# Grouped-query decode attention on one core: half of the first values between the first keys, the last pair's values in the loop

## The chip, the cores and the metric

The kernel runs on one core of a Trainium2 chip. The metric is the device time of one execution in microseconds (us). The core has TensorE (matrix products), VectorE, ScalarE and GpSimd (elementwise work, reductions, copies), SyncE (which here issues nearly all transfers) and 16 DMA engines that move data between the chip's HBM memory and the core's SBUF. TensorE writes its results to PSUM.

## The reference

One query token attends to 65,536 keys. There are 32 query heads and 8 key and value heads, so 4 query heads share each key head; a head has 128 elements, all in bf16.

```
scale = D ** -0.5                                   # D = 128
scores = jnp.einsum("bhqd,bhkd->bhqk", q, k) * scale
p = _softmax(scores, axis=-1)
return jnp.einsum("bhqk,bhkd->bhqd", p, v)          # k, v repeated 4 times over heads
```

Keys and values are 134 MB each; every byte is used once, for four queries.

## The kernel before, in words

**Tiles.** A head's 65,536 keys are cut into 4 units of 16,384 keys. A unit lies in SBUF as 128 partitions by 128 tiles (T) of 128 elements: 4.19 MB. Two units are a *pair*; there are 16 pairs (NP), two per head. Below, Kp and Vp are the keys and the values of pair p, and a and b their first and second unit.

**Buffers.** `kbuf` holds two units, `vbuf` two, `bbuf` one. A pair's keys are loaded as one transfer into kbuf (pairs 1 to 14, `WHOLE`), and GpSimd (6 of 8 blocks, L223) and ScalarE (2 blocks, L347) copy the second unit from kbuf to bbuf, so that kbuf comes free for the next pair's keys early. Pairs 0 and 15 are loaded a unit at a time, straight to kbuf's first half and to bbuf.

**One lap of a pair.** TensorE transposes each key tile (L138) so that the head's elements lie along the partitions, eight tiles at a time; VectorE (three of four groups, L217) and ScalarE (one of four, L215) move the transposed tiles from PSUM to SBUF; TensorE multiplies them with the four queries (L149). VectorE takes the maximum over the pair (L237), GpSimd over partitions (L386); ScalarE takes the exponentials (L340) into `pts`, and their sums. After the keys of a lap, TensorE multiplies the exponentials of the *previous* pair with its values (`pe_values`, L154 to L161): 256 products in one PSUM group, opened by the first product. So V(p) is used in lap p+1. VectorE then adds the PSUM result to the head's running sum `acc`: a copy for the first pair of a head (L281), a product with alpha, the correction for a new maximum (L294), an addition for the second pair (L285), and the division by the sum of exponentials (L286).

**The loop and what follows it.** TensorE's loop has 16 laps (L195). It skips the values in lap 0. The last pair's values come behind the loop, in code of their own (`pe_last_values`, L163 to L175), from kbuf; there the running sum enters the PSUM group as a product with an identity matrix (L169). Ahead of the loop are 48 small products (`PE_LEAD`, L190).

**Order of the transfers.** SyncE's program is written out (L433 to L447) and is executed in order: a wait holds up all that is behind it. The transfers run in one queue, in order of issue. The order is K0 in four pieces, K1, V0, K2, V1, and so on to K15, V14, V15. Each is held by a wait: K(p) for `kfree` (L409), three tokens per pair: one when the first unit has been transposed, one from GpSimd and one from ScalarE when their copies are done; a unit into bbuf for `bfree`, when bbuf has been transposed; V(p) for `vfree` (L430), when the values before it have been summed. V15 goes into kbuf, its second unit in four pieces (`L_PIECES`, 78, 32, 13 and 5 tiles), so that little work is left behind the last one. The results of 7 heads are stored from `orow`, those of the last head from `lrow` (L447).

Of the kernel before, what the change touches and what calls it, by code (L numbers as in the profile page):

```python
# [7 lines left out]
ALU = mybir.AluOpType  # L8
# [3 lines left out]
T = 128  # L12
# [4 lines left out]
LAG = 3  # L17


PE_LEAD = 48  # L20
CB = 16
HU = 4
Q = 32


K_PIECES = ((64, 64), (64, 64))
L_PIECES = ((128,), (78, 32, 13, 5))

# [11 lines left out]
def starts(sizes):  # L42
    return [sum(sizes[:i]) for i in range(len(sizes))]


def take(e, sem, n=1):

    e.wait_ge(sem, n)
    e.sem_inc(sem, -n)  # L49


def bass_standalone__gqa_softmax__decode_kernel(nc, q, k, v, out):
    _, Hq, _, D = q.shape
    _, H, Sk, _ = k.shape
    R = Hq // H
# [13 lines left out]
    def sem(name):  # L69
        return S(nc.semaphore(name))  # L70
# [36 lines left out]
    qps = pvb[1][:, :].bitcast(DT.bfloat16)  # L107

    kp = [[sem(f"kp{i}_{p}") for p in range(len(K_PIECES[i]))] for i in range(2)]
    vp = sem("vp")  # L110
    lvp = [[sem(f"lvp{i}_{p}") for p in range(len(L_PIECES[i]))] for i in range(2)]

    kfree, bfree = sem("kfree"), sem("bfree")
    cpg, cpa, pgo = sem("cpg"), sem("cpa"), sem("pgo")
# [36 lines left out]
        if j == G - 1:  # L151
            ins.then_inc(qkd, 1)

    def pe_values(pe):  # L154
        vv = vbuf[:, :].rearrange("p (t d) -> p t d", d=D)
        take(pe, vp, 16)
        for n in range(2):
            for t in range(T):
                ins = pe.matmul(pvb[0][:, 0:R], lhsT=vv[:, n * T + t, :], rhs=pts[n][:, t * R:(t + 1) * R],  # L159
                                start=n == 0 and t == 0, stop=n == 1 and t == T - 1)  # L160
            ins.then_inc(pvd if n else pfree, 1)  # L161

    def pe_last_values(pe):  # L163
        vv = kbuf[:, :].rearrange("p (t d) -> p t d", d=D)
        for n in range(2):
            pe.wait_ge(exd, n + 1)
            if n:
                pe.wait_ge(acr, H)
                pe.matmul(pvb[1][:, 0:R], lhsT=identf[:, :], rhs=acc[:, :], start=False, stop=False)  # L169
            for t in range(T):  # L170
                if t in starts(L_PIECES[n]):
                    pe.wait_ge(lvp[n][starts(L_PIECES[n]).index(t)], 16)
                ins = pe.matmul(pvb[1][:, 0:R], lhsT=vv[:, n * T + t, :], rhs=pts[n][:, t * R:(t + 1) * R],  # L173
                                start=n == 0 and t == 0, stop=n == 1 and t == T - 1)
        ins.then_inc(pvd, 1)  # L175

    def pe_keys(pe):
        pend = []
# [9 lines left out]
    def tensor_engine(pe):  # L188
        pe.wait_ge(t_id, 1)
        for _ in range(PE_LEAD):  # L190
            pe.matmul(pvb[0][0:R, 0:R], lhsT=ident[:, 0:R], rhs=ident[:, 0:R], start=True, stop=True)
        pe.wait_ge(q_sem, 16)
        pe.transpose(qps[:, 0:HR], qsb[:, :], ident[0:HR, 0:HR]).then_inc(s_x, 1)
        pe.wait_ge(t_if, 1)
        with pe.Fori(0, NP) as lap:  # L195
            pe_keys(pe)
            with pe.If(lap > 0):
                pe_values(pe)
        pe_last_values(pe)
        pe.wait_ge(t_f, 1)  # L200
        pe.transpose(trb[0][0:R, 0:P], oT[:, HR - R:HR], ident[:, :]).then_inc(s_x, 1)  # L201

# [62 lines left out]
    def dve_pair(e, second, lap):  # L265

        for n in range(2):
            for j in range(G):
                if not on_act(j):
                    evict(e, n, j)  # L270
                if n == 0 and j == 0:
                    e.sem_inc(pgo, 1)
        pair_max(e)
        if second:
            next_queries(e)
        else:
            e.sem_inc(qrdy, 1)
        new_max(e, second)
        if second:
            values_done(e)  # L280
            own(e, e.tensor_copy(acc[:, :], pvb[0][:, 0:R]), xd)  # L281
        else:
            with e.If(lap > 0):
                values_done(e)
                own(e, e.tensor_tensor(acc[:, :], acc[:, :], pvb[0][:, 0:R], ALU.add), xd)  # L285
                own(e, e.tensor_tensor(oT[:, HR - R:HR], acc[:, :], recip[:, :], ALU.mult), xd)  # L286
                own(e, e.tensor_copy(otmp[:, 0:HR - R], oT[:, R:HR]), xd)
                own(e, e.tensor_copy(oT[:, 0:HR - R], otmp[:, 0:HR - R]), xd)
                e.transpose(orow[:, :], oT[:, :]).then_inc(t_o, 1)
        take(e, sx)  # L290
        if not second:
            own(e, e.tensor_tensor(lp[:, :], rsum[:, 0:R], rsum[:, R:2 * R], ALU.add), xd)
            return
        own(e, e.tensor_tensor(acc[:, :], acc[:, :], alpha[:, :], ALU.mult), xd)  # L294
        own(e, e.tensor_tensor(lp[:, :], lp[:, :], alpha[:, :], ALU.mult), xd)
        for n in range(2):
            own(e, e.tensor_tensor(lp[:, :], lp[:, :], rsum[:, n * R:(n + 1) * R], ALU.add), xd)
        e.sem_inc(acr, 1)
        e.sem_inc(lrd, 1)
        take(e, lra)  # L300
        own(e, e.reciprocal(recip[:, :], la[:, :]), xd)
# [16 lines left out]
    def vector_engine(e):  # L318
        make_identity(e)
        e.memset(oT[:, :], 0.0)  # L320
        e.memset(dm[:, :], 0.0)
        e.wait_ge(s_x, 1)
        own(e, e.tensor_copy(qT[:, :], qps[:, 0:HR]), xd)
        next_queries(e)
        with e.Fori(0, H) as lap:
            dve_pair(e, False, lap)
            dve_pair(e, True, lap)
        e.wait_ge(pvd, 1)
        e.tensor_tensor(oT[:, HR - R:HR], pvb[1][:, 0:R], recip[:, :], ALU.mult).then_inc(t_f, 1)  # L329
        e.wait_ge(s_x, 2)  # L330
        e.tensor_copy(lrow[:, :], trb[0][0:R, 0:P]).then_inc(t_row, 1)  # L331

# [11 lines left out]
    def act_pair(e, lap):  # L344

        def copy(o, i):
            return e.activation(o, i, AF.Copy)  # L347

        for j in (3, 7, 11, 15):
            evict(e, 0, j)  # L350
            if j in ACT_COPIES:
                copy_unit(e, (lap - (WHOLE[0] - 1)) * (WHOLE[1] - lap) > 0, ACT_COPIES[j], copy, cpa, xa)
                if j == max(ACT_COPIES):
                    e.sem_inc(kfree, 1)
        for j in (3, 7, 11, 15):
            evict(e, 1, j)
        for n in range(2):
            take(e, pfree)
            exps(e, n)
        take(e, dmr)  # L360
        e.activation(alpha[:, :], dm[:, :], AF.Exp, scale=1.0).then_inc(sx, 1)
# [29 lines left out]
    def sync_engine(e):  # L391
        W = T * D

        def src(x, p):
            h, c = p // 2, p % 2
            return x[h, c * 2 * P * T:(c + 1) * 2 * P * T, :].rearrange("(p t) d -> p (t d)", p=P)

        def pieces(to, s, sizes, sems):
            for a, w, sm in zip(starts(sizes), sizes, sems):
                e.dma_start(to[:, a * D:(a + w) * D], s[:, a * D:(a + w) * D]).then_inc(sm, 16)  # L400

        def tokens(sems):
            for sm in sems:
                e.sem_inc(sm, 16)

        def keys(p):
            ks = src(kf, p)
            if p:
                e.wait_ge(kfree, 3 * p)  # L409
            if WHOLE[0] <= p < WHOLE[1]:  # L410
                e.dma_start(kbuf[:, :], ks).then_inc(kp[0][0], 16)
                tokens(kp[0][1:])
                e.wait_ge(bfree, p)
                tokens(kp[1])
                return
            for n in range(2):
                if n and p:
                    e.wait_ge(bfree, p)
                to, s = bbuf if n else kbuf, ks[:, n * W:(n + 1) * W]
                if p == 0:  # L420
                    pieces(to, s, K_PIECES[n], kp[n])
                else:
                    e.dma_start(to[:, 0:W], s).then_inc(kp[n][0], 16)
                    tokens(kp[n][1:])
            e.sem_inc(cpg, len(POOL_COPIES))
            e.sem_inc(cpa, len(sum(ACT_COPIES.values(), ())))

        def values(p):
            if p:
                e.wait_ge(vfree, p)  # L430
            e.dma_start(vbuf[:, :], src(vf, p)).then_inc(vp, 16)

        keys(0)  # L433
        for p in range(1, NP):
            keys(p)
            values(p - 1)
        e.wait_ge(kfree, 3 * NP)
        vs = src(vf, NP - 1)
        for n in range(2):
            pieces(kbuf[:, n * W:(n + 1) * W], vs[:, n * W:(n + 1) * W], L_PIECES[n], lvp[n])  # L440
        e.wait_ge(t_o, H - 1)
        for b, rows in enumerate(OUT_ROWS):
            for r, n in zip(starts(rows), rows):
                e.dma_start(of[r:r + n, b * Q:(b + 1) * Q],
                            orow[b * Q + r:b * Q + r + n, :]).then_inc(o_sem, 16)
        e.wait_ge(t_row, 1)
        e.dma_start(of[HR - R:HR, :], lrow[:, :]).then_inc(l_sem, 16)  # L447
# [37 lines left out]
```

## Time and profile before

| What | Value |
|---|---|
| Time, median of 3 runs | 628.31 us (628.17 to 630.41) |
| Profiled execution: time, and its span | 630.51 us, 629.1 us |
| TensorE, VectorE, ScalarE, GpSimd busy | 77%, 49%, 37%, 26% of the span |
| Moved by DMA | 268.60 MB, 427 GB/s over the span |
| Granted TensorE clock, mean | 0.774 |

The span is the time from the first to the last instruction that the profiler saw. A group of instructions is named by the line that issued it, the engine, and the tiles that it writes and reads; a "busy" TensorE may still wait inside. "q1" and so on are DMA queues; "instruction" queues carry the engines' code. The letter q behind an engine's name (SPq) is its sequencer, which issues transfers and holds waits.

### The profile page before, as it was taken

To read this page: it belongs to the slowest core of one execution; us is meant where nothing else is said; L and a number is where in the kernel's file an instruction comes from. 1 tells how busy PE (TensorE), PEld (TensorE's weight loads), DVE (VectorE), ACT (ScalarE), POOL (GpSimd) and SP (SyncE) were. 2 spreads that over 40 slices of the span, in tenths; PEclk is the share of its full clock that TensorE was granted. 3 is DMA by queue.
4 is the path that set the end of the run, shared out by engine and by line. 5 is a ranking of instruction groups with operands and counts; after the bars stand their busy time and mean duration, and the time that the engine had idled before them with its cause. 6 is when DMAs were issued, how large, how long until landed. Compare 5 with 4: busy or idle time off the path is not lost. (4 is left out here: it accounts for less than half of the span.)

```text
span 629.1 us, 27597 instructions
## 1 busy us (share of the span) xinstructions
PE 483.7 (77%) x12340; PEld 479.1 (76%) x12340; DVE 306.2 (49%) x608; ACT 234.2 (37%) x431; POOL 165.0 (26%) x114
## 2 busy tenths in 40 slices
PE   5749869497695967949689494995949859599975
PEld 5749869497695967949689494994949859499965
DVE  4627447173461735627355372643717437174730
ACT  2235333263432634325243252433525334253321
POOL 0007051060611506024070340703307042070000
PEclk9958769596695967859678596786959869597975
DMA  8999999999999999999999999999999999999996
GB/s 367 428 419 434 433 438 429 438 433 433 433 433 429 446 421 446 425 442 425 442 425 442 425 442 425 442 425 442 425 442 425 442 429 438 429 421 430 454 405 277
DMA packets 5994, 268.60 MB, mean 427 GB/s; under 512 B 864, under 2 KB 992, under 8 KB 1120
## 3 DMA queue, kind: packets, MB, share of 16 engines
q1 hardware_dynamic: 5936, 268.45, 99.0%
q8 instruction: 8, 0.13, 0.1%
q10 hardware_dynamic: 48, 0.01, 0.0%
q14 instruction: 2, 0.02, 0.0%
HBM read 268.44 MB, written 0.01 MB: 427 GB/s over the span
## 5 line engine op out<-in xcount | busy, mean ns | idle before, releaser
L217 DVE COPY ktb<-trb 128x1024 bf16<-128x1024 bf16 x384 | 257.1, 692 | 169.4 <-PE trb L138 166.7
L138 PE MATMUL trb<-ident,kbuf 128*128 128x128 bf16 x2048 | 178.0, 245 | 115.5 <-PEq L49 115.5
L215 ACT ACTIVATE ktb<-trb 128x1024 bf16<-128x1024 bf16 x128 | 131.1, 1024 | 284.2 <-PE trb L138 230.0
L138 PEld LDWEIGHTS trb<-ident,kbuf 128*128 128x128 bf16 x2048 | 144.8, 111 | 116.4 <-issue 116.4
L223 POOL COPY bbuf<-kbuf 128x2048 bf16<-128x2048 bf16 x84 | 154.9, 1893 | 132.3 <-POOLq L49 132.3
L149 PE MATMUL qkb<-qcur,ktb 128*128 128x4 bf16 x4096 | 173.6, 165 | 12.5 <-PEq L49 11.7
L149 PEld LDWEIGHTS qkb<-qcur,ktb 128*128 128x128 bf16 x4096 | 155.6, 97 | 15.1 <-issue 14.3
L138 PE MATMUL trb<-ident,bbuf 128*128 128x128 bf16 x2048 | 157.3, 220 | 3.1 <-issue 3.1
L138 PEld LDWEIGHTS trb<-ident,bbuf 128*128 128x128 bf16 x2048 | 117.8, 97 | 3.3 <-issue 3.3
L159 PE MATMUL pvb<-pts,vbuf 128*128 128x4 bf16 x3840 | 103.4, 166 | 3.9 <-PEq L49 3.9
L159 PEld LDWEIGHTS pvb<-pts,vbuf 128*128 128x128 bf16 x3840 | 102.5, 102 | 4.2 <-issue 4.0
L340 ACT ACTIVATE pts<-qkb,negm 128x128 bf16<-128x128 f32 x128 | 50.9, 546 | 95.7 <-ACTq L49 95.7
L386 POOL PARTITION_ALL_REDUCE cmaxa<-cmaxp x16 | 5.9, 371 | 247.4 <-POOLq L49 247.4
L347 ACT ACTIVATE bbuf<-kbuf 128x2048 bf16<-128x2048 bf16 x28 | 53.3, 1902 | 0.0
L340 ACT ACTIVATION_READ_ACCUMULATOR pts<-qkb,negm 128x1 f32 x128 | 34.9, 272 | 0.0
L237 DVE TENSOR_REDUCE cmax<-qkb 128x4 f32<-128x512 f32 x32 | 22.0, 687 | 17.4 <-DVEq L49 17.4
L388 POOL PARTITION_ALL_REDUCE la<-lp x8 | 3.4, 429 | 72.8 <-POOLq L49 72.8
L281 DVE COPY acc<-pvb 128x4 f32<-128x4 f32 x8 | 1.3, 162 | 42.0 <-DVEq L263 42.0
L285 DVE TENSOR_TENSOR acc<-acc,pvb 128x4 f32<-128x4 f32 x7 | 1.1, 158 | 34.5 <-DVEq L263 34.5
L173 PE MATMUL pvb<-pts,kbuf 128*128 128x4 bf16 x256 | 7.5, 166 | 4.9 <-DMA kbuf<-in_v_dram 4.9
L173 PEld LDWEIGHTS pvb<-pts,kbuf 128*128 128x128 bf16 x256 | 7.2, 104 | 5.2 <-ACT pts L340 2.8
L294 DVE TENSOR_TENSOR acc<-acc,alpha 128x4 f32<-128x4 f32 x8 | 1.3, 163 | 11.6 <-DVEq L49 11.6
(46 smaller groups left out, 38.2 us busy)
## 6 DMA issues: line engine op xcount, KB each, us to landing
kbuf<-in_k_dram SPq DMA_DIRECT2D x2, 2048.0 KB, 9.6
bbuf<-in_k_dram SPq DMA_DIRECT2D x2, 2048.0 KB, 19.9
kbuf<-in_k_dram SPq DMA_DIRECT2D x1, 4096.0 KB, 16.2
bbuf<-in_k_dram SPq DMA_DIRECT2D x1, 4096.0 KB, 16.5
kbuf<-in_v_dram SPq DMA_DIRECT2D x1, 4096.0 KB, 25.4
kbuf<-in_v_dram SPq DMA_DIRECT2D x1, 2496.0 KB, 31.0
kbuf<-in_v_dram SPq DMA_DIRECT2D x1, 1024.0 KB, 33.0
kbuf<-in_v_dram SPq DMA_DIRECT2D x1, 416.0 KB, 33.5
```

What stands on the lines that cost most here:

```text
L138: ins = pe.transpose(trb[j % NTB][:, i * P:(i + 1) * P], kv[:, t, :], ident[:, :])
L149: ins = pe.matmul(qkb[n][:, t * R:(t + 1) * R], lhsT=ktb[:, off:off + P], rhs=qcur[:, :], start=True, stop=True)
L159: ins = pe.matmul(pvb[0][:, 0:R], lhsT=vv[:, n * T + t, :], rhs=pts[n][:, t * R:(t + 1) * R], start=n == 0 and t == 0, stop=n == 1 and t = ...
L173: ins = pe.matmul(pvb[1][:, 0:R], lhsT=vv[:, n * T + t, :], rhs=pts[n][:, t * R:(t + 1) * R], start=n == 0 and t == 0, stop=n == 1 and t = ...
L215: e.activation(dst, trb[j % NTB][:, :], AF.Copy).then_inc(eva, 1)
L217: e.tensor_copy(dst, trb[j % NTB][:, :]).then_inc(evd, 1)
L223: ins = op(bbuf[:, c * CB * D:(c + 1) * CB * D], kbuf[:, off:off + CB * D])
L237: ins = e.tensor_reduce(cmax[:, n * R:(n + 1) * R], qkb[n][:, :].rearrange("p (t g) -> p g t", g=R), AX.X, ALU.max)
L340: ins = e.activation(pv[:, g, :], sv[:, g, :], AF.Exp, bias=negm[:, g:g + 1], scale=scale, accum_out=rsum[:, n * R + g:n * R + g + 1])
L347: return e.activation(o, i, AF.Copy)
L386: e.partition_all_reduce(cmaxa[:, :], cmaxp[:, :], P, bass.bass_isa.ReduceOp.max).then_inc(cma, 1)
L388: e.partition_all_reduce(la[:, :], lp[:, :], P, bass.bass_isa.ReduceOp.add).then_inc(lra, 1)
```

## The change

**Loads.** SyncE's order becomes K0a, V0a, K0b, K1, V0b, K2, V1, and on as before. K0b is one transfer instead of two pieces. V0a and V0b have no wait of their own; V0b comes behind K1's two waits. At the end V15b is loaded first, whole, into kbuf's first half, and V15a in four pieces (73, 33, 15 and 7 tiles) into vbuf's first half. The pieces wait for a new semaphore, `vhalf`, which ScalarE raises once per lap when the first half of the previous pair's values has been used.

**TensorE.** The loop has 17 laps. The keys are skipped in the last one, the values in the first. One function does a pair's values in all laps: it waits for `acc` (`acr`), opens the PSUM group with the product of `acc` and the identity matrix, then multiplies. In lap 16 it takes V15b from kbuf, then V15a from vbuf, in pieces; in the others V(p)a and V(p)b from vbuf. Some products stand twice in the code for that. `pe_last_values` goes, and PE_LEAD becomes 8.

**VectorE.** For the first pair of a head `acc` is set to zero; for the second it is the PSUM result times alpha, in one operation. The copy and the addition go.

The diff, cut to its core:

```diff
-PE_LEAD = 48
+PE_LEAD = 8
-K_PIECES = ((64, 64), (64, 64))
-L_PIECES = ((128,), (78, 32, 13, 5))
+K_PIECES = ((64, 64), (128,))
+V_PIECES = ((73, 33, 15, 7), (128,))
...
+    def pe_values(pe, buf, ps, sems, tiles=range(T), stop=False):
+        vv = buf.rearrange("p (t d) -> p t d", d=D)
+        for t in tiles:
+            piece = sems.get(t)
+            if piece:
+                pe.wait_ge(piece, 16)
+            ins = pe.matmul(pvb[0][:, 0:R], lhsT=vv[:, t, :], rhs=ps[:, t * R:(t + 1) * R],
+                            start=False, stop=stop and t == tiles[-1])
+            if piece:
+                pe.sem_inc(piece, -16)
+        return ins
+
+    def pe_pair_values(pe, lap):
+        first, second = (vbuf[:, n * T * D:(n + 1) * T * D] for n in range(2))
+        sems = [dict(zip(starts(V_PIECES[n]), vp[n])) for n in range(2)]
+        most, rest = range(T - V_PIECES[0][-1]), range(T - V_PIECES[0][-1], T)
+        take(pe, acr)
+        pe.matmul(pvb[0][:, 0:R], lhsT=identf[:, :], rhs=acc[:, :], start=True, stop=False)
+        with pe.If(lap == NP):
+            pe.wait_ge(exd, 2)
+            pe_values(pe, kbuf[:, 0:T * D], pts[1], {0: lvp})
+        pe_values(pe, first, pts[0], sems[0], most)
+        with pe.If(lap < NP):
+            pe_values(pe, first, pts[0], sems[0], rest).then_inc(pfree, 1)
+            pe_values(pe, second, pts[1], sems[1], stop=True).then_inc(pvd, 1)
+        with pe.Else():
+            pe_values(pe, first, pts[0], sems[0], rest, stop=True).then_inc(pvd, 1)
...
-        with pe.Fori(0, NP) as lap:
-            pe_keys(pe)
+        with pe.Fori(0, NP + 1) as lap:
+            with pe.If(lap < NP):
+                pe_keys(pe)
             with pe.If(lap > 0):
-                pe_values(pe)
-        pe_last_values(pe)
+                pe_pair_values(pe, lap)
...
             values_done(e)
-            own(e, e.tensor_copy(acc[:, :], pvb[0][:, 0:R]), xd)
...
-                own(e, e.tensor_tensor(acc[:, :], acc[:, :], pvb[0][:, 0:R], ALU.add), xd)
-                own(e, e.tensor_tensor(oT[:, HR - R:HR], acc[:, :], recip[:, :], ALU.mult), xd)
+                own(e, e.tensor_tensor(oT[:, HR - R:HR], pvb[0][:, 0:R], recip[:, :], ALU.mult), xd)
...
         if not second:
+            e.memset(acc[:, :], 0.0).then_inc(acr, 1)
...
-        own(e, e.tensor_tensor(acc[:, :], acc[:, :], alpha[:, :], ALU.mult), xd)
+        e.tensor_tensor(acc[:, :], pvb[0][:, 0:R], alpha[:, :], ALU.mult).then_inc(acr, 1)
...
         for n in range(2):
             take(e, pfree)
+            if n == 0:
+                e.sem_inc(vhalf, 1)
             exps(e, n)
...
-        keys(0)
-        for p in range(1, NP):
+        key_unit(0, 0)
+        value_unit(0, 0)
+        key_unit(0, 1)
+        copied()
+        keys(1)
+        value_unit(0, 1)
+        for p in range(2, NP):
             keys(p)
             values(p - 1)
         e.wait_ge(kfree, 3 * NP)
         vs = src(vf, NP - 1)
-        for n in range(2):
-            pieces(kbuf[:, n * W:(n + 1) * W], vs[:, n * W:(n + 1) * W], L_PIECES[n], lvp[n])
+        e.dma_start(kbuf[:, 0:W], half(vs, 1)).then_inc(lvp, 16)
+        e.wait_ge(vhalf, NP)
+        pieces(vbuf[:, 0:W], half(vs, 0), V_PIECES[0], vp[0])
```

`keys(p)` waits as before, for kfree and bfree; `key_unit` and `value_unit` issue one unit's transfer.

More of the change, by code (lines that the diff above doesn't have):

```diff
@@ L109, in bass_standalone__gqa_softmax__decode_kernel @@
     kp = [[sem(f"kp{i}_{p}") for p in range(len(K_PIECES[i]))] for i in range(2)]
-    vp = sem("vp")
-    lvp = [[sem(f"lvp{i}_{p}") for p in range(len(L_PIECES[i]))] for i in range(2)]
+    vp = [[sem(f"vp{i}_{p}") for p in range(len(V_PIECES[i]))] for i in range(2)]
+    lvp, vhalf = sem("lvp"), sem("vhalf")
     kfree, bfree = sem("kfree"), sem("bfree")
@@ L152, in pe_scores @@
             ins.then_inc(qkd, 1)
-    def pe_values(pe):
-        vv = vbuf[:, :].rearrange("p (t d) -> p t d", d=D)
-        take(pe, vp, 16)
-        for n in range(2):
[L158 to L175, printed above, removed]
+    def pe_values(pe, buf, ps, sems, tiles=range(T), stop=False):
[9 more added lines that the diff above has]
+        return ins
@@ L297, in dve_pair @@
             own(e, e.tensor_tensor(lp[:, :], lp[:, :], rsum[:, n * R:(n + 1) * R], ALU.add), xd)
-        e.sem_inc(acr, 1)
         e.sem_inc(lrd, 1)
@@ L328, in vector_engine @@
         e.wait_ge(pvd, 1)
-        e.tensor_tensor(oT[:, HR - R:HR], pvb[1][:, 0:R], recip[:, :], ALU.mult).then_inc(t_f, 1)
+        e.tensor_tensor(oT[:, HR - R:HR], pvb[0][:, 0:R], recip[:, :], ALU.mult).then_inc(t_f, 1)
         e.wait_ge(s_x, 2)
@@ L404, in tokens, with half, key_unit, copied @@
                 e.sem_inc(sm, 16)
+        def half(x, n):
+            return x[:, n * W:(n + 1) * W]
+        def key_unit(p, n):
+            to, s = (bbuf if n else kbuf)[:, 0:W], half(src(kf, p), n)
+            if p == 0:
+                pieces(to, s, K_PIECES[n], kp[n])
+            else:
+                e.dma_start(to, s).then_inc(kp[n][0], 16)
+                tokens(kp[n][1:])
+        def copied():
+            e.sem_inc(cpg, len(POOL_COPIES))
+            e.sem_inc(cpa, len(sum(ACT_COPIES.values(), ())))
         def keys(p):
-            ks = src(kf, p)
-            if p:
-                e.wait_ge(kfree, 3 * p)
+            e.wait_ge(kfree, 3 * p)
             if WHOLE[0] <= p < WHOLE[1]:
-                e.dma_start(kbuf[:, :], ks).then_inc(kp[0][0], 16)
+                e.dma_start(kbuf[:, :], src(kf, p)).then_inc(kp[0][0], 16)
                 tokens(kp[0][1:])
@@ L415, in keys, with value_unit @@
                 return
[L416 to L426, printed above, removed]
-        def values(p):
-            if p:
-                e.wait_ge(vfree, p)
-            e.dma_start(vbuf[:, :], src(vf, p)).then_inc(vp, 16)
-        keys(0)
-        for p in range(1, NP):
+            key_unit(p, 0)
+            e.wait_ge(bfree, p)
+            key_unit(p, 1)
+            copied()
+        def value_unit(p, n):
+            e.dma_start(half(vbuf, n), half(src(vf, p), n)).then_inc(vp[n][0], 16)
+            tokens(vp[n][1:])
+        def values(p):
+            e.wait_ge(vfree, p)
+            e.dma_start(vbuf[:, :], src(vf, p)).then_inc(vp[0][0], 16)
+            tokens(vp[0][1:])
+            tokens(vp[1])
+        key_unit(0, 0)
+        value_unit(0, 0)
+        key_unit(0, 1)
+        copied()
+        keys(1)
+        value_unit(0, 1)
+        for p in range(2, NP):
             keys(p)
@@ L438, in sync_engine @@
         vs = src(vf, NP - 1)
-        for n in range(2):
-            pieces(kbuf[:, n * W:(n + 1) * W], vs[:, n * W:(n + 1) * W], L_PIECES[n], lvp[n])
+        e.dma_start(kbuf[:, 0:W], half(vs, 1)).then_inc(lvp, 16)
+        e.wait_ge(vhalf, NP)
+        pieces(vbuf[:, 0:W], half(vs, 0), V_PIECES[0], vp[0])
         e.wait_ge(t_o, H - 1)
```

## The prediction

> **What bounds the kernel now.** I read the page's second and third part first (what is busy, and what the transfers do), then the windows of the trace, the issues on SyncE's queue in order of time, and last the timeline around the start and the end.
>
> ```profile
> span 629.1 us, 27597 instructions
> ...
> DMA  8999999999999999999999999999999999999996
> ...
> q1 hardware_dynamic: 5936, 268.45, 99.0%
> q8 instruction: 8, 0.13, 0.1%
> ```
>
> The transfers are busy in every slice but the first and the last, and the queue that carries keys and values (q1) takes 99.0% of the span. No engine comes near that. So the time is: what passes before the DMA queue is full, 268 MB at the queue's rate, every moment in which the queue is empty, and what is left after the last byte.
>
> ```profile
> 70.00:590.00 520.00, 0.77 1.00 433
> 0.00:4.00 4.00, 1.00 0.61 194
> 4.00:18.00 14.00, 1.00 1.01 428
> 18.00:20.00 2.00, 1.00 0.96 410
> 20.00:30.00 10.00, 1.00 1.03 419
> ```
>
> Columns: the window, its length, TensorE's granted clock, the DMA share, GB/s. In the middle it is 433 GB/s at share 1.00: nothing to gain there. One unit (half a pair, 4.194 MB) takes 4.194 / 433 = 9.7 us, a pair of units 19.4 us; one lap moves 16.8 MB, 38.7 us. There are 64 units. The middle is full because SyncE issues ahead of need; how far ahead is the question on which this change turns.
>
> ```profile
> 20.55 0.33 SPq L411 DMA_DIRECT2D kbuf<-in_k_dram  x1
> 37.17 0.33 SPq L431 DMA_DIRECT2D vbuf<-in_v_dram  x1
> 58.70 0.33 SPq L411 DMA_DIRECT2D kbuf<-in_k_dram  x1
> 77.17 0.33 SPq L431 DMA_DIRECT2D vbuf<-in_v_dram  x1
> ```
>
> Call pair p's keys Kp and its values Vp; a and b are the first and second unit. These are the issues of K1, V0, K2 and V1.
>
> ```profile
> 46.06 3.57 PE L138 MATMUL trb<-ident,kbuf 128*128 128x128 bf16 x32 [7.46 <-PEq L49]
> 84.76 3.57 PE L138 MATMUL trb<-ident,kbuf 128*128 128x128 bf16 x32 [7.77 <-PEq L49]
> 47.40 11.07 POOL L223 COPY bbuf<-kbuf 128x2048 bf16<-128x2048 bf16 x6 [6.65 <-POOLq L49]
> ...
> SPq L411 <- POOLq L384: 264.3, 13, 21.2
> ```
>
> TensorE starts on K1 at 46.06 and on K2 at 84.76; since it waits before both, these are the landings as an engine sees them. K2 goes into the buffer that holds K1, so SyncE waits until GpSimd has copied K1's second unit out of it (13 of the 14 whole loads wait for that, L384). The chain is fixed: K1 seen at 46.06, copies 47.40 to 58.47, K2 issued at 58.70, which is **12.64 us after K1 is seen**. In those 12.64 us the queue lives on V0, 19.4 us long. It has 19.4 - 12.64 = 6.7 us to spare, less what a new transfer needs to begin.
>
> **The change part by part.**
>
> *V0a between K0a and K0b.* It costs no byte. First, what it removes. By the windows 7.8 MB had moved when K1 was issued at 20.55 (0.78 + 5.99 + 0.82 + 0.24); 0.56 MB, 1.3 us, were left. A transfer on an empty queue takes longer than its bytes:
>
> ```profile
> DMA to landing us min/median/max: 7.4/25.4/33.5
> DMA to landing us min/median/max: 25.4/25.9/26.0
> ```
>
> The first row is L400: the first 2.1 MB landed 7.4 us after issue, 2.6 us more than the 4.84 their bytes take. The second is L411: K1's 8.39 MB, its minimum, 25.4, is 6.0 over its 19.4. Of those 6.0, 1.3 were K0's rest. So K1 came too late to keep all rings busy, and some of its delay goes once V0a and K0b lie ahead of it. That gain g is at least 0 and at most 6.0 - 1.3 = 4.7; I take 2.0, nearer the 2.6 of the transfer that began on an empty queue.
>
> What it adds. K1 now has five units up to its end instead of four, so TensorE sees it at 46.06 + 9.7 - 2.0 = 53.8. But behind K1 only V0b is queued, one unit, 9.7 us, where it was two. K2 still comes 12.64 us after K1 is seen. **The queue runs dry:** V0b is all down about 9.7 us after K1, and K2 is issued some 3 us later than that and needs its start on top. This stall is not in the trace of before; it follows from 12.64 against 9.7, two lengths that are there, and the edit touches neither the copies nor the wait.
>
> To this comes the code of the first lap. TensorE starts K0b only when all of it is there (K_PIECES is now one piece), about 9.7 us later than it had K0, and that half lap took 18.2 us (20.44 to 38.61) with a stall in it that no engine and no transfer of data ended:
>
> ```profile
> 20.44 0.61 PE L138 MATMUL trb<-ident,bbuf 128*128 128x128 bf16 x8
> ...
> 31.91 0.71 PE L138 MATMUL trb<-ident,bbuf 128*128 128x128 bf16 x5 [3.10 <-issue]
> ...
> 38.25 0.36 PE L149 MATMUL qkb<-qcur,ktb 128*128 128x4 bf16 x8 [0.74 <-PEq L49]
> ...
> q8 instruction: 6, 0.10, 0.6%
> ```
>
> The last row is the DMA view of 0 to 60: six loads of code, by which I read that stall as a wait for code. So it ends its first keys at 47 to 52 (it may start near 20.44 + 9.7 + 2 = 32; to this 15 to 18 us and up to 2 for a cold clock), and then branches past the values to the end of the loop, code it has not had yet. Before, the same branch lay in the 7.46 us of waiting for K1. One such load may end after 53.8: 0 to 4 us, and I take 0.7. TensorE begins K1 at 54.5, and K2 is issued at 54.5 + 12.64 = 67.1.
>
> K2 on an empty queue: at least 19.4 + 2.6 = 22.0 us until it is seen; at most what K1 took less K0's rest, (46.06 - 20.55) - 1.3 = 24.2. I take the middle, 23.0, as both rows have half of the conditions. TensorE begins K2 at 90.1, where it was 84.76. At that point both versions have moved the same eight units, and after it both have the same sequence. So the step is **+5.4 us** at the end. Both ends: g of 4.7 and a 22.0 us load give 46.06 + 9.7 - 4.7 + 12.64 + 22.0 = 85.7, +0.9; no g, 4 us of code and 24.2 give 96.6, +11.8.
>
> [...]
>
> *Does V1 follow in time?* It is issued when the values of pair 0 are summed: 77.17 - 46.06 = 31.1 us after K1 is seen, so at 54.5 + 31.1 + 0.5 = 86.1 with the additions below, 4 us before K2 is seen and 1.4 us before its bytes end by the 2.6 above. That is just enough; if the first pass through the values also waits for code, up to 3 us are added. I take 0. From there a lap is as before: two units of values cover 12.64 us, and nothing accumulates.
>
> *Sums that open each PSUM group.*
>
> ```profile
> L281 DVE COPY acc<-pvb 128x4 f32<-128x4 f32 x8 | 1.3, 162 | 42.0 <-DVEq L263 42.0
> ...
> 620.44 0.57 PE L169 MATMUL pvb<-acc,identf 128*128 128x4 f32 x2
> ...
> 78.93 0.16 DVE L294 TENSOR_TENSOR acc<-acc,alpha 128x4 f32<-128x4 f32 x1 [1.45 <-DVEq L49]
> 108.43 6.91 PE L159 MATMUL pvb<-pts,vbuf 128*128 128x4 bf16 x256
> ```
>
> VectorE loses 8 copies of 162 ns and 7 additions of the same shape (L285, taken at the same), 2.4 us, and gets 8 clears of that shape, at most as long. TensorE gets 16 identity products, 0.57 us each at half clock, 9 us over all laps, and about ten semaphore instructions per lap. Neither is on the path: TensorE waits 7.5 to 8 us per lap for keys. The wait for acr has the values queued behind it, and vbuf's freeing behind these; but acc is multiplied by alpha at 78.93, and the values that now wait for it start at 108.43, so it is there. If that cover is gone, a values load is issued as much later, against some 7 us to spare in a steady lap. I count nothing.
>
> *PE_LEAD 48 to 8.*
>
> ```profile
> 3.26 1.34 PE L191 MATMUL pvb<-ident 128*4 128x4 bf16 x48 [3.26 <-DVE ident L315]
> 8.22 3.57 PE L138 MATMUL trb<-ident,kbuf 128*128 128x128 bf16 x32 [2.95 <-PEq L49]
> ```
>
> These 1.34 us of products lie ahead of the query and of the keys at 8.22, for which TensorE waits 2.95 us. Nothing; if the clock fell by it, K0a would be done a few us later, and K1 now has two units ahead of it.
>
> *The last pair in the loop, and its loads.*
>
> ```profile
> 591.46 2.23 SPq L400 DMA_DIRECT2D kbuf<-in_v_dram  x5
> ...
> 607.31 6.97 PE L159 MATMUL pvb<-pts,vbuf 128*128 128x4 bf16 x256 [3.94 <-PEq L49]
> 611.07 0.55 ACT L340 ACTIVATE pts<-qkb,negm 128x128 bf16<-128x128 f32 x1 [8.18 <-ACTq L49]
> 617.03 3.56 PE L173 MATMUL pvb<-pts,kbuf 128*128 128x4 bf16 x128 [2.75 <-DMA kbuf<-in_v_dram]
> ```
>
> Before, all five loads were queued at 593.7. Now V15b is, and V15a's four pieces wait for vhalf, which ScalarE gives when it begins these exponentials: 611.07 here. Behind the wait on SyncE lie the results' stores alone. V15b is seen at 617.03, so the pieces come 6.0 us ahead of its landing and the 2.6 us to begin fit: nothing, with 3.4 us to spare.
>
> ```profile
> 625.38 1.72 PE L173 MATMUL pvb<-pts,kbuf 128*128 128x4 bf16 x50 [0.23 <-DMA kbuf<-in_v_dram]
> 627.14 0.16 DVE L329 TENSOR_TENSOR oT<-pvb,recip 128x4 bf16<-128x4 f32 x1 [8.63 <-PE pvb L173]
> ...
> q8 instruction: 2, 0.03, 0.4%
> ```
>
> The last piece grows from 5 to 7 tiles: 2 x 1.72 / 50 = 0.07 us. The last row is the DMA view of 600 to 629.1: two loads of 16 KB of code for what followed the loop, beside the last values; on one of 16 rings (27 GB/s) each takes 0.6 us. If they hit the ring that ends last that is 1.2 us, if not 0; I take 0.4. End: -0.3 us.
>
> **Sum:** +5.4 - 0.3 = +5.1 us. The profiled execution took 630.51 us with a span of 629.1; the span would be 634.2. The median of the three runs is 628.31, 2.2 below the profiled one; with the same step, 628.31 + 5.1 = 633.4 us.
>
> **The rivals.**
>
> *The gap closes and none opens* (not slower). V0a fills the gap at K1, and K2 still meets a filled queue. Decisive is whether K2 can be issued by 9.7 - 2.6 = 7.1 us after K1 is seen. Price: -2.0 - 0.3, 626.0 us; at the full 4.7, 623.3. Against it: 11.07 us of copies alone are more than 7.1. Chance 0.06, half of it below 625.2.
>
> *The stall is there but small:* rings in step after V0a, no wait for code, a quick start of K2. Terms near their low ends, +0.6 to +3.1: 629 to 631.4. Chance 0.09.
>
> *The loop's code does not stay* (the change does not do what it says). Between 60 and 600 us the DMA view has no code on q8, so a lap's 768 matrix products all stayed in TensorE. Now a lap's code holds 905 (128 + 7 + 2 more, and no longer behind the loop). If that is over what TensorE keeps, each lap loads it again. Priced by lap 0: a stall of 3.10 at one load, and at least eight loads for the lap (0.13 MB came in 8). TensorE is busy 29.8 us of 38.7:
>
> ```profile
> q1 hardware_dynamic: 4162, 233.97, 100.1%
> q14 instruction: 1, 0.01, 0.0%
> ...
> sum 77.00, PE 59.58 PEld 59.05 DVE 38.04 ACT 29.99 POOL 23.30; mean PE 29.79 PEld 29.53 DVE 19.02 ACT 14.99 POOL 11.65
> ```
>
> (first the queues from 60 to 600, then two laps' sums). With eight full stalls 29.8 + 24.8 = 54.6, 15.9 over the DMA's lap, 240 us in 15 laps: about 870; with half of them, about 680. [...] Chance 0.13.
>
> **How the numbers follow.** The forecast, a stall at K2 of over 3 us, has 0.72; the rivals 0.06, 0.09 and 0.13. Predicted is the forecast's 633.4. Its own range, from its middle bounds, is 631 to 639; to hold 8 in 10 it takes in the small stall, 629.8 to 639, and leaves out reloaded code, a closed gap and the far ends. About 0.5%, 3.1 us, is what a measurement here can tell from no change: faster 0.03, same 0.12, slower 0.85.
>
> **What would show it.** SyncE's third whole issue (K2) should stand at 66 to 70, its landing seen by TensorE at 88 to 94, and the windows between 60 and 70 should hold a hole of DMA share well under 1. The windows from 100 to 600 should stay at 433 GB/s. At 20 to 30 the rate should be full. The DMA view of 100 to 590 should have no code on q8; if it has, the third rival is at work. If K2 is issued by 61, or the queue has no hole there, the main step is wrong; if the hole is there and the time is not longer, the queue was not the bound.

## The result, and the profile after

The changed kernel takes **846.91 us** (median of 6 runs, 843.35 to 852.16) against 629.26 us for the kernel before (6 runs): a ratio of 1.3463, 95% interval 1.3408 to 1.3517. The forecast was 633.4 us with a range to 639; what came is the third rival, the loop's code that does not stay, priced there at 680 to 870.

The page of the changed kernel: the span, what the engines do, the DMA row in 40 slices, and the queues that carry data (q1) and TensorE's code (q8).

```profile
span 843.1 us, 27731 instructions
...
PE 532.2 (63%) x12330; PEld 521.7 (62%) x12330; DVE 305.0 (36%) x601; ACT 233.8 (28%) x431; POOL 165.0 (20%) x114
...
DMA  9975599596986949769497893968959698684945
...
q1 hardware_dynamic: 5936, 268.45, 75.4%
q8 instruction: 137, 2.24, 1.0%
```

The same 268.45 MB in the same 5936 packets now fill 75.4% of the span instead of 99.0%. The slices of 9 in a row are gone: the DMA row alternates. And q8 has 137 loads where it had 8. Their 2.24 MB are 1.0% of the DMA's time, so the code does not crowd out the data; something waits for it. The DMA view of 60 to 600 us, where the kernel before had no load on q8:

```profile
q1 hardware_dynamic: 3021, 173.34, 75.9%
q8 instruction: 91, 1.49, 1.1%
```

Who waits, in the view of waits for TensorE (idle us in total, times, longest):

```profile
PE pvb L160 <- issue: 116.2, 45, 7.1
PE trb L138 <- PEq L49: 75.6, 17, 12.1
PE qkb L149 <- issue: 60.4, 25, 4.5
PE trb L138 <- issue: 33.6, 15, 3.7
```

"issue" is idle time that nothing in the profile ends: no data, no engine. Here it is 210 us. Before, all of TensorE's "issue" was 3.9 us, in two rows:

```profile
PE trb L138 <- issue: 3.1, 1, 3.1
...
PE qkb L149 <- issue: 0.8, 1, 0.8
```

One lap of the changed kernel in the timeline shows the pattern, which returns in every lap at the same products (L160 are values, L138 and L149 keys):

```profile
409.27 1.76 PE L160 MATMUL pvb<-pts,vbuf 128*128 128x4 bf16 x57 [5.61 <-issue]
412.34 3.49 PE L160 MATMUL pvb<-pts,vbuf 128*128 128x4 bf16 x125 [1.32 <-issue]
415.99 2.12 PE L160 MATMUL pvb<-pts,vbuf 128*128 128x4 bf16 x74 [0.16 <-issue]
422.07 3.57 PE L138 MATMUL trb<-ident,kbuf 128*128 128x128 bf16 x32 [3.96 <-PEq L49]
...
434.49 0.33 PE L138 MATMUL trb<-ident,kbuf 128*128 128x128 bf16 x3 [1.47 <-issue]
...
441.93 0.18 PE L149 MATMUL qkb<-qcur,ktb 128*128 128x4 bf16 x1 [2.44 <-issue]
...
449.09 0.33 PE L149 MATMUL qkb<-qcur,ktb 128*128 128x4 bf16 x7 [0.54 <-issue]
```

Groups of eight products are cut in two (5 and 3, 7 and 1, 1 and 7): the stop has nothing to do with their work. The first and longest wait, 5.61 us, comes where the lap branches past the 128 products of the last pair; the one at 422.07 where the loop returns to its start (its keys were issued 36 us earlier and were down). Together 15.5 us per lap. The windows of the same lap show what this does to the transfers (columns as in the prediction, with TensorE's busy time ahead):

```profile
387.00:407.00 20.00, 12.55 (x262) 0.76 0.96 412
407.00:419.00 12.00, 7.36 (x256) 0.50 0.02 5
419.00:437.00 18.00, 13.46 (x268) 0.79 1.05 439
```

```profile
385.54 0.33 SPq L429 DMA_DIRECT2D kbuf<-in_k_dram  x1
418.29 0.33 SPq L445 DMA_DIRECT2D vbuf<-in_v_dram  x1
435.60 0.33 SPq L429 DMA_DIRECT2D kbuf<-in_k_dram  x1
```

The keys issued at 385.54 are down by 407. The next load needs the values' buffer, which TensorE frees late, at 418.29; for 12 us the queue is empty. Then it runs at its full 439 GB/s. A lap is 50 to 52 us (385.54 to 435.60, and 52.3 to the issue after) instead of 38.7. **TensorE, held up by its own code, has become the bound**, and the DMA queue, which was the bound, waits for it.

### The profile page after: what moved, and what is told of

Its sections match the earlier page's. It is cut to its first block, busy times and chain, and to the rows that moved or that the text cites. A ratio compares the mean times of both kernels' runs of the same rounds, so it can differ in the third digit from the quotient of the medians.

```text
span 843.1 us, 27731 instructions
## 1 busy us (share of the span) xinstructions
PE 532.2 (63%) x12330; PEld 521.7 (62%) x12330; DVE 305.0 (36%) x601; ACT 233.8 (28%) x431; POOL 165.0 (20%) x114
## 3 DMA queue, kind: packets, MB, share of 16 engines
q1 hardware_dynamic: 5936, 268.45, 75.4%
q8 instruction: 137, 2.24, 1.0%
## 5 line engine op out<-in xcount | busy, mean ns | idle before, releaser
L138 PE MATMUL trb<-ident,kbuf 128*128 128x128 bf16 x2048 | 184.4, 248 | 97.1 <-PEq L49 63.6
L149 PE MATMUL qkb<-qcur,ktb 128*128 128x4 bf16 x4096 | 181.4, 166 | 72.2 <-issue 60.4
L149 PEld LDWEIGHTS qkb<-qcur,ktb 128*128 128x128 bf16 x4096 | 165.6, 101 | 76.0 <-issue 75.7
L138 PEld LDWEIGHTS trb<-ident,kbuf 128*128 128x128 bf16 x2048 | 148.1, 112 | 99.9 <-issue 99.9
L138 PE MATMUL trb<-ident,bbuf 128*128 128x128 bf16 x2048 | 182.3, 241 | 12.1 <-PEq L49 12.1
L160 PE MATMUL pvb<-pts,vbuf 128*128 128x4 bf16 x3968 | 114.1, 166 | 116.2 <-issue 116.2
L160 PEld LDWEIGHTS pvb<-pts,vbuf 128*128 128x128 bf16 x3968 | 110.6, 104 | 119.7 <-issue 119.6
L138 PEld LDWEIGHTS trb<-ident,bbuf 128*128 128x128 bf16 x2048 | 137.4, 108 | 12.2 <-issue 12.2
L171 PE MATMUL pvb<-acc,identf 128*128 128x4 f32 x32 | 8.3, 330 | 7.0 <-PEq L49 7.0
L171 PEld LDWEIGHTS pvb<-acc,identf 128*128 128x128 f32 x32 | 7.4, 287 | 7.0 <-issue 7.0
```

Of the source, the lines that this page charges most:

```text
L138: ins = pe.transpose(trb[j % NTB][:, i * P:(i + 1) * P], kv[:, t, :], ident[:, :])
L149: ins = pe.matmul(qkb[n][:, t * R:(t + 1) * R], lhsT=ktb[:, off:off + P], rhs=qcur[:, :], start=True, stop=True)
L160: ins = pe.matmul(pvb[0][:, 0:R], lhsT=vv[:, t, :], rhs=ps[:, t * R:(t + 1) * R], start=False, stop=stop and t == tiles[-1])
L171: pe.matmul(pvb[0][:, 0:R], lhsT=identf[:, :], rhs=acc[:, :], start=True, stop=False)
```

## The experiments

The theory: the loop's code no longer stays in TensorE, is loaded again in each lap, and the time goes into waiting for it. The rivals: the waits for `acc`, which now opens each group; the new order of loads; the 17th lap and its branches. Each ratio below is against the kernel before, timed beside it.

**The last pair behind the loop again** (5 runs). Of the change, the loads, the sums and the short PE_LEAD stay.

```diff
-        with pe.Fori(0, NP + 1) as lap:
-            with pe.If(lap < NP):
-                pe_keys(pe)
+        with pe.Fori(0, NP) as lap:
+            pe_keys(pe)
             with pe.If(lap > 0):
                 pe_pair_values(pe, lap)
+        pe_pair_values(pe, None)       # None: the last pair's branch alone
```

> The changed kernel with the last pair's values behind the loop again; the loads, the sums that open the PSUM group and the short PE_LEAD stay. Theory code (the loop's code no longer stays in TensorE and is loaded again in each lap): some 8 loads of code in all instead of 137, none between 100 and 590 us, and the time falls from 847 to near the kernel before, plus what the new order of loads costs, 629 + 5 = 634 us. Rival sums (TensorE waits in each lap for acc, which now opens the group): the time stays near 847 us, since that wait is kept. Rival loads (the new order of loads keeps the queue from running ahead in every lap): stays near 847 us too.

Measured: 650.59 us, ratio 1.0355 (1.033 to 1.038). Ten loads of code, none of them between 110 and 600 us. So 196 of the 218 us go with the place of that code; rivals sums and loads fall as the main cause, since both were kept. But it is 22 us over the kernel before, not 5: something else costs too.

**Code alone** (1 run). Nothing of the change, but as many products in the loop as it has.

```diff
-PE_LEAD = 48
+PE_LEAD = 8
...
             with pe.If(lap > 0):
                 pe_values(pe)
+            with pe.If(lap < 1):
+                for _ in range(137):
+                    pe.matmul(pvb[1][0:R, 0:R], lhsT=ident[:, 0:R], rhs=ident[:, 0:R], start=True, stop=True)
```

> The kernel before with nothing of the change but code: PE_LEAD 8, and 137 small products in the loop that only lap 0 executes (some 4 us, while TensorE waits for the second pair's keys anyway) and the other laps branch past. They write a part of PSUM that is overwritten later. Theory code: the loop has as many products as the changed one, so it is loaded again in each lap, over 100 loads of code, and the time goes to 800 to 870 us. Rivals sums and loads: within 2 us of the kernel before, since neither is touched.

Measured: 840.22 us. Its page has

```profile
q8 instruction: 138, 2.26, 1.2%
```

That is the loss of the change without its loads, sums, laps or branches: 15 laps of it never execute the added code. The theory stands. What it does not say is how much code is too much, so three kernels looked for the edge, with the theory *size*: how much code the loop holds decides whether it stays.

**32 and 88 unused products** (1 run each), the same edit with other counts:

> The kernel before with PE_LEAD 8 and 32 unused products in the loop (lap 0 alone executes them, into a part of PSUM that is overwritten later) where the run of code alone had 137. [...] Rival: any further branch in the loop makes it load again, over 100 loads and 800 us or more.

> [...]

Measured: 634.36 us with 32 and 833.35 us with 88. First the row of code loads with 32, then three rows of the run with 88: its loads, and the unused products in lap 0.

```profile
q8 instruction: 10, 0.16, 0.1%
```

```profile
42.58 1.64 PE L201 MATMUL pvb<-ident 128*4 128x4 bf16 x60 [6.72 <-issue]
49.64 0.84 PE L201 MATMUL pvb<-ident 128*4 128x4 bf16 x28 [5.42 <-issue]
...
q8 instruction: 137, 2.24, 1.2%
```

The second row shows where a load begins: after 60 of the 88 products TensorE waits 5.42 us for it. A load is 16 KB (2.24 MB in 137). How much code that is, TensorE's stops tell. With PE_LEAD 8, counted in the order of the code from TensorE's first product, they stand after 215, 336 and 458 products (lap 0 of the first run above: 1.78, 3.68 and 2.03 us), after 582 and 710 (behind 61 and 189 of the first values with PE_LEAD 8 alone, rows below: 4.11 and 3.45 us), and after 837 here (521 up to the end of the keys, 256 values and 60). These are 121 to 128 products apart. So, as an estimate, one load brings the code of 121 to 128 products, and I count a loop in stretches of that length; the one that ends at 215 is taken to begin at 94, where the first ends. Nine products lie ahead of the loop, so it begins in the first. With 32 it ends at 809, in the seventh stretch, and its time is that of PE_LEAD 8 alone (634.79, below); between 110 and 600 us it loads no code. With 88 it ends at 865, 28 products into the eighth; the run shows 137 loads, 83 of them between 110 and 600 us.

**A long PE_LEAD** (10 runs) asks whether it is the place in the program or the extent of the loop.

```diff
-PE_LEAD = 48
+PE_LEAD = 150
```

> The kernel before with PE_LEAD 150 and nothing else; the 102 added products end before the first keys are there. [...]

Measured: 628.39 us, ratio 0.9992 (0.9974 to 1.0011), and

```profile
q8 instruction: 9, 0.15, 0.1%
```

This loop ends later in the program than the one with 88, after 919 products instead of 865, by the same estimate in the eighth stretch too, but it begins at 151, in the second. So it is not the place of the end that decides: by the estimate the loops in seven stretches stayed at both places, and those in eight did not. The runs do not tell stretches from products. The largest loop that stayed (the smaller change, next) has 809 products and the smallest that did not (88 unused) has 856, so a limit in products between the two would fit as well. In the changed kernel a lap makes 9 loads (370 to 422.07 us, and 422.07 to 474.3), one more than its loop has stretches by the estimate; why is not shown.

**The change, smaller** (1 run): 96 products left out.

```diff
-        most, rest = range(T - V_PIECES[0][-1]), range(T - V_PIECES[0][-1], T)
+        most, rest = [t for t in range(T - V_PIECES[0][-1]) if not 41 <= t < 73], range(T - V_PIECES[0][-1], T)
...
-            pe_values(pe, kbuf[:, 0:T * D], pts[1], {0: lvp})
+            pe_values(pe, kbuf[:, 0:T * D], pts[1], {0: lvp}, range(96))
...
-            pe_values(pe, second, pts[1], sems[1], stop=True).then_inc(pvd, 1)
+            pe_values(pe, second, pts[1], sems[1], range(96), stop=True).then_inc(pvd, 1)
```

> [...] Loads, sums, 17 laps and all branches stay. Theory size: no code between 110 and 600 us, and the time falls to 640 to 655 us, near the run with the last pair behind the loop and a short lead. Rival: 17 laps and the branches of the last one cost by themselves, over 700 us.

Measured: 647.46 us, with

```profile
q8 instruction: 8, 0.13, 0.1%
```

A lap executes 64 products fewer, some 1.8 us of TensorE's time (125 take 3.49 us in the lap shown above); the time fell by 199 us. The 17 laps and the branches stayed, so that rival falls too.

**The loads alone** (5 runs): the step on which the forecast rested.

```diff
+        def half_values(n):
+            e.dma_start(vbuf[:, n * W:(n + 1) * W], src(vf, 0)[:, n * W:(n + 1) * W]).then_inc(vp[n], 16)
...
                 if p == 0:
                     pieces(to, s, K_PIECES[n], kp[n])
+                    if n == 0:
+                        half_values(0)
...
-            if p:
-                e.wait_ge(vfree, p)
+            if p == 0:
+                half_values(1)
+                return
+            e.wait_ge(vfree, p)
```

> The kernel before with the new order of the first loads alone: half of pair 0's values between the first and second unit of pair 0's keys, the other half behind pair 1's keys. The step of the prediction (the queue runs dry before pair 2's keys): 629 + 5, between 632 and 638 us, with a hole in the DMA's share between 60 and 70 us. Rival: the gap at pair 1's keys closes and none opens, 626 to 628 us. Rival loads of the first run: 840 us.

Measured: 635.91 us, ratio 1.0114 (1.0093 to 1.0134): 7.5 us slower. Its windows, then the issue of K2 and TensorE's starts on K1 and K2:

```profile
50.00:60.00 10.00, 4.56 (x52) 0.50 1.00 424
60.00:64.00 4.00, 4.00 (x95) 0.89 0.15 66
64.00:70.00 6.00, 6.00 (x152) 1.00 0.52 175
...
100.00:600.00 500.00, 393.97 (x10105) 0.77 1.00 433
```

```profile
55.44 3.57 PE L138 MATMUL trb<-ident,kbuf 128*128 128x128 bf16 x32 [7.23 <-PEq L49]
68.08 0.33 SPq L414 DMA_DIRECT2D kbuf<-in_k_dram  x1
90.05 3.57 PE L138 MATMUL trb<-ident,kbuf 128*128 128x128 bf16 x32 [3.65 <-PEq L49]
```

The hole is there, once, between 60 and 70, and the rest runs at 433 GB/s. K2 is issued 12.64 us after K1 is seen, as before.

**K1's second unit early** (12 runs): the same gap at K1 closed without taking V0 from behind it.

```diff
+                if p == 1:
+                    e.dma_start(kbuf[:, W:2 * W], ks[:, W:2 * W]).then_inc(k1b, 16)
                 e.wait_ge(kfree, 3 * p)
             if WHOLE[0] <= p < WHOLE[1]:
-                e.dma_start(kbuf[:, :], ks).then_inc(kp[0][0], 16)
+                part = slice(0, W if p == 1 else 2 * W)
+                e.dma_start(kbuf[:, part], ks[:, part]).then_inc(kp[0][0], 16)
```

(The copies out of kbuf's second half wait for k1b.)

> The kernel before with one load moved: the second unit of pair 1's keys goes to kbuf's second half, which is free from the start, ahead of the wait for the first half; so the queue holds a unit more when the first half is issued, and two units of values still lie behind pair 1's keys. If the gap at pair 1's keys costs what the prediction took (2 us, at most 4.7): 624.5 to 627.5 us. Rival: the gap lies on rings that are not the last ones: within 0.5 us of the kernel before.

Measured: 629.13 us against 628.39, ratio 1.0005 (0.9991 to 1.0019): no difference. In its trace K2 is issued earlier, at 57.01 where it was 58.70:

```profile
57.01 0.33 SPq L415 DMA_DIRECT2D kbuf<-in_k_dram  x1
```

The start came 1.7 us sooner in the profiled execution, and the timed runs do not show it; why not stays open.

**PE_LEAD 8 alone**, and **the first run above with PE_LEAD 48** (4 runs each) ask for its other 15 us.

```diff
-PE_LEAD = 48
+PE_LEAD = 8
```

> The kernel before with PE_LEAD 8 instead of 48 and nothing else. The first run with the last pair behind the loop was 15 us over the one with the new loads alone, and its TensorE stood still for code in laps 0 and 1. Theory place: the 40 products fewer move the code, so that other places of lap 0 wait for a load; here the second whole load of keys may come 0 to 6 us later than 58.7 and the time is 628 to 635 us. Rival sums: PE_LEAD alone changes nothing, within 1 us of the kernel before, and the 15 us come from the sums or the last loads.

> The changed kernel with the last pair's values behind the loop and PE_LEAD 48 again: the new loads and the sums that open the PSUM group stay. Theory place: the waits for code in laps 0 and 1 fall as in the run with the new loads alone, and the time is near that run, 634 to 640 us. Rival sums: it stays near 650 us.

Measured: 634.79 us, ratio 1.0080 (1.0047 to 1.0113), for PE_LEAD 8 alone; 638.06 us, 1.0153 (1.0123 to 1.0183), with the change's loads and sums and PE_LEAD 48. So a short PE_LEAD costs 5.9 us by itself and 12.5 beside the new loads. Of the 22 us of the first run, 7.5 then go with the new loads and 12.5 with the short lead; some 2 are left. The values in lap 1, first before and then with PE_LEAD 8 alone:

```profile
70.12 6.87 PE L159 MATMUL pvb<-pts,vbuf 128*128 128x4 bf16 x256
```

```profile
74.79 3.58 PE L159 MATMUL pvb<-pts,vbuf 128*128 128x4 bf16 x128 [4.11 <-issue]
81.81 1.95 PE L159 MATMUL pvb<-pts,vbuf 128*128 128x4 bf16 x67 [3.45 <-issue]
```

```profile
83.94 0.33 SPq L431 DMA_DIRECT2D vbuf<-in_v_dram  x1
```

The first pass through the values waits twice for code, and V1 is issued at 83.94 instead of 77.17. The delay was expected at K2, but K2 was issued at 57.86, earlier than before (58.70); by 80 it is all but down, and the queue is nearly empty until V1 comes (the window from 80 to 84):

```profile
80.00:84.00 4.00, 1.95 (x67) 0.50 0.18 70
```

Behind the loop and with the short lead (the first run) both delays add: TensorE was 8.7 us later on K1 than with the loads alone, and waited again in the first values:

```profile
64.09 3.19 PE L138 MATMUL trb<-ident,kbuf 128*128 128x128 bf16 x32 [6.76 <-PEq L49]
...
97.69 2.06 PE L160 MATMUL pvb<-pts,vbuf 128*128 128x4 bf16 x71 [3.59 <-issue]
```

None of these kernels beats the kernel before by more than its interval.

## Why the prediction was wrong, point by point

- **The step that failed is the assumption that the loop's code stays**, given as the rival *The loop's code does not stay* with a chance of 0.13. It counted the products right (905 against 768) and named the sign to look for, code on q8 between 100 and 590. But that 905 would stay too was the author's estimate, and with it the chance stayed small. No row of before showed what size stays beyond the 768 products of its own loop. The runs put the edge between a loop of 809 products and one of 856: the changed loop makes 137 loads of code and stands still for them in each lap, which makes TensorE the bound. The step costs 196 us (846.91 against 650.59).
- **Its price came near by luck.** Stalls of 24.8 us per lap were set, 8 full ones; the lap shown has 15.5, in seven of very different length, and the two laps from 370 to 474.3 leave TensorE idle 17.9 us each. With that the prediction's own sum (29.8 + 17.9 against 38.7, 15 laps) gives some 760 us. But TensorE was also busy longer, 34.3 us per lap in these two where 29.8 was taken. The mean clock was lower too (0.711 against 0.774); how much of the busy time goes with that was not tested. 870 was said and 847 came because one term was too large and the other too small.
- ***V0a between K0a and K0b* was right, mechanism and place.** With the loads alone K1 was seen at 55.44 (said: 54.5), K2 issued at 68.08 (67.1) and seen at 90.05 (90.1, where before it was 84.76). Within this, two terms were mis-sized against each other: g, 2.0 and the code of lap 0, 0.7, should have given 1.3 us earlier than 46.06 + 9.7; it was 0.3, and which of the two was off is not shown. K2 then took 21.97 us (68.08 to 90.05), the lower bound, where 23.0 was taken. That K1 came 0.9 us later and K2 took 1.0 us less than said, so that 90.05 meets 90.1, is luck.
- **The time of that run was 7.5 us over before**, where the prediction's step is 5.4 (its -0.3 at the end belongs to code and loads that this run does not change). V15a is seen 5.9 us later than before (622.91 against 617.03), but the second unit's first piece 7.2 us later (630.10 against 622.91). From 605 us to the end TensorE has no wait for code in either kernel (no row there waits for issue), so why the last pieces came later still stays open.
- ***PE_LEAD 48 to 8* was costed at nothing and costs 5.9 us.** What was priced was the products' own 1.34 us and a lower clock. What the edit also does is to move all code behind it, and with it the places where laps 0 and 1 wait for a load: in lap 0 after 289 and 411 of its products before, after 206 and 449 with PE_LEAD 8 alone. The prediction has "if the first pass through the values also waits for code, up to 3 us are added. I take 0". With PE_LEAD 8 alone it does wait, 4.11 and 3.45 us.
- **The sums that open each group, and the last pair's loads, were costed at nothing, and no clear cost was found.** With both, and the new loads, and PE_LEAD 48, 638.06 us stand against 635.91 with the loads alone; the intervals (1.0123 to 1.0183, and 1.0093 to 1.0134) overlap, but a cost of some 2 us is not excluded.
- **The gain at K1, up to 4.7 us, is worth nothing that can be measured** where it was taken alone.

## What to carry to other kernels

Count the products of a loop before code is moved into it: here loops of up to 809 products stayed in TensorE and one of 856 did not, and with 56 unused products more (88 against 32) the kernel took 199 us longer (833.35 against 634.36). If a step has such an edge and no row shows on which side it falls, the edge deserves the larger chance. And before a transfer is moved ahead, ask what it was covering: the two units of V0 covered the 12.64 us from K1's landing to K2's issue, and one unit, 9.7 us, does not.

## What the runs showed of the hardware that was not expected

- Loops of 856 and 905 products were loaded again lap after lap: 137 loads in all with 88 unused products, 83 of them between 110 and 600 us; 138 with 137 unused, 84 of them there; 137 in the changed kernel, 9 in its lap from 422.07 to 474.3. Loops of 768, 800 and 809 products made no load between 110 and 600 us.
- One such load is 16 KB (2.24 MB in 137), but TensorE's waits in the changed kernel are 0.2 to 7.1 us, in the lap shown longest behind a branch past code that is not executed (5.61 us at 409.27).
- 40 products fewer ahead of a loop (PE_LEAD 8) cost 5.9 us, with waits for code of 4.11 and 3.45 us in lap 1 that the kernel before does not have; 102 more (PE_LEAD 150) cost nothing, 0.9992 (0.9974 to 1.0011).
